# Weighted copies and normalisation products of an attention kernel: from VectorE to GpSimd, with 66 in place of 67 rows and a new order

## The chip, the cores and the metric

The kernel runs on one core of a Trainium2 chip. The metric is the device time of the whole program in microseconds, lower is better; times are medians over several executions. Durations and waits come from one profiled execution. The engines are called as in the profile: PE (TensorE, matrix products; PEld is its loading of weights), ACT (ScalarE), DVE (VectorE), POOL (GpSimd) and SP (SyncE, which here issues DMAs); ACTq and SPq are the engines' sequencers issuing DMAs.

## The reference

A block of multi-head attention: 2048 positions, width 448, 16 heads of 28.

```python
def reference(x, wqkv, wo):
    B, S, D = x.shape
    H = 16
    Dh = D // H
    qkv = (lambda x, *d: x.transpose(*d))((x @ wqkv).reshape(B, S, 3, H, Dh), 2, 0, 3, 1, 4)
    q, k, v = qkv[0], qkv[1], qkv[2]
    scores = jnp.einsum("bhqd,bhkd->bhqk", q, k) * (Dh ** -0.5)
    p = _softmax(scores, axis=-1)
    o = jnp.einsum("bhqk,bhkd->bhqd", p, v)
    return (lambda x, *d: x.transpose(*d))(o, 0, 2, 1, 3).reshape(B, S, D) @ wo
```

All inputs are bfloat16.

## The kernel before, in words

**Tiles, rows, units.** The 16 heads are four groups `g` of four; the 2048 queries are four chunks `c` of 512. A pair (g, c) is a *unit*; there are 16, in the order g then c, so units 12 to 15 are the last group. Within a unit the keys are 16 blocks `kt` of 128. A *tile* is the scores of 128 keys by 512 queries of one head (one PSUM bank); four tiles, one for each head of the group, are a *row*. So there are 256 rows of four tiles, numbered 16 u + kt.

**Two ways to an exponential.** Most tiles go to ACT, which reads two or three banks at once and writes exponentials in bfloat16 to `PT` (line 966). The rows named in `PLAN["rows"]` (line 347) go to DVE in place of that: PE computes each of the four tiles into a bank of its own, DVE turns it into an int16 whose bits, read as a 16-bit float, are a first approximation of the exponential (`DY`, `row_tile`, line 928), and two more instructions over the whole row add a constant phase each (`DS`, line 936). The three are summed with weights 1, 101/128 and 80/128. PE does that sum in the product with V: where a row of ACT needs one pass over V, a row of DVE needs three, the first with `V` and the others with the weighted copies `VW` of it (line 871, function `pv`). The copies are made per group and quarter of the keys, two instructions each (lines 857 to 862): 4 x 4 x 2 = 32 in all. `VW` holds two groups, so a third group's copies wait for the last readers of the first (`vw_used`).

**Banks.** Five of the eight PSUM banks alternate between a three-wide and a two-wide group for ACT, and the tiles for ACT are dealt out 3, 2, 3, 2 and so on (lines 639 to 663). The end of the list is cut so that the last item is one tile wide, in a bank of its own (lines 660 to 663). The other three banks (pool "M", line 508) carry everything else: the sum over V of the current unit, the tiles for DVE, the projections, the output projection.

**End of a unit** (`post_unit`, line 719). DVE copies the sum from PSUM to `OTS` (line 723). The row sums of the softmax are one of its columns; they go by two small DMAs through memory into another layout (L1, L2, lines 729 and 731), DVE takes reciprocals (line 733), and two more DMAs (L3, L4, lines 735 and 737) bring these back, repeated over the partitions, into `RB`. Then `OTS` is multiplied by `RB` into `OTN` (line 739, on the engine `NMENG`, line 372). This holds for units 0 to 13. Unit 14 (`norm_pe`) and unit 15 (`last_unit`) spread the reciprocals with PE and multiply on DVE. When the unit belongs to the last group, four output tiles of its chunk follow: four products with `wop` (line 710), an evacuation (line 696 on ACT, line 698 on DVE) and a store (line 700). Of the last unit's four tiles, 12 to 15, ACT evacuates 12 and 14, DVE 13 and 15; the store of a tile that ACT evacuated is issued by ACT, the others by SP.

**The order.** Every engine executes one list, written out by a planner when the program is built (`_Prog.schedule`, line 125). It takes each operation with its dependencies, a booked duration (`dur`), a priority (`prio`) and, where needed, a bank, and simulates the engines. `CFG` (line 344) holds its settings and `PLAN` the rows and the priorities ("late") of the projections of later groups. Once the lists stand, each engine runs its own strictly in order and waits on semaphores where a producer is on another engine. Where PE has nothing to do the planner puts in products with zeros (line 484).

Beside all this stands a second, general version of the kernel, entered only if a check on the reciprocals fails; it isn't run with these inputs.

Of the kernel before, what the change touches and what calls it, by code (L numbers as in the profile page):

```python
# [63 lines left out]
class _Prog:  # L64
# [276 lines left out]
ZLO = -ZADD  # L341


CFG = {"late": 4.5, "load": 1.5, "load0": 18, "dcost": 2.3, "dlead": 30.385592406, "aslack": 235.147215477, "opp": 0.0, "oload": 2.5, "klead": 0.405674492, "vlag": 0.024622608, "hot1": 45000.0, "hotm": 3600.0, "nslack": 2585.717981114, "dlook": 20.0, "plook": 471.074451806, "rcost": 4.9, "rlead": 1.0, "rend": 4, "rgap": 2, "acost": 0.4455, "dprio": 0.651412491, "nride": 4, "rslack": 300.0, "stail": 24, "jprio": -0.750113813, "sdlap": 4.771128299, "vwlead": 1.249363626, "sdpen": 6.528606395, "rcostx": -0.000676632}

PLAN = {
    "rows": [9, 14, 16, 24, 26, 28, 33, 38, 41, 50, 53, 54, 57, 61, 62, 70, 72, 77, 80, 84, 88, 95, 97, 98, 103, 107, 109, 111, 113, 117, 123, 125, 131, 135, 138, 139, 141, 148, 149, 152, 162, 163, 164, 165, 169, 176, 177, 179, 180, 187, 189, 190, 193, 199, 200, 207, 211, 212, 213, 215, 222, 229, 231, 234, 235, 244, 248],
    "late": [1.281070854, 1.964014751, 1.915657661, 0.76, 2.743900482, 1.159356603, 1.904466413, 1.845975994, 2.106524837, 2.189415295, 2.428349574, 2.873971098, 2.728623137, 3.84085501, 2.733578841, 4.131340808, 3.508351422, 5.446684044, 4.832243098, 4.46548081, 5.163206443, 7.002171665, 6.90767575, 7.804407036, 4.947925744, 6.78739139, 5.302922841, 6.89552453, 9.777227448, 10.389677342, 7.735503962, 7.490566717, 8.23514301, 7.360578973, 7.83742904, 10.319692841, 8.329224918, 8.680463746],
}


def _fast(nc, x, wqkv, wo, out, n_heads=16):
# [9 lines left out]
    NK = NST  # L362
    QCH = 512
    NCH = S // QCH
    NQT = QCH // 128
# [3 lines left out]
    NDR = 3  # L369
    NDS = 3  # L370
    NPH = len(PHASE)
    NMENG = "dve"
    NOB = 4
    scale = float(DH) ** -0.5
    VONE = DH
# [5 lines left out]
    of = out.rearrange("b s d -> (b s) d")  # L381
# [4 lines left out]
    P = _Prog()  # L386
    es = ExitStack()
    with es:
# [66 lines left out]
        def dma_of(t, g):  # L455
# [12 lines left out]
        def zero_pass(acc_open, t):  # L468
# [12 lines left out]
            def emit(e):  # L481
                ins = None
                for h in range(4):
# [13 lines left out]
                       deps=[id_f_op], dur=100, prio=-6, name="sel")  # L497
# [34 lines left out]
        xt_ev = {}  # L532
# [29 lines left out]
        v_ev, vw_ev, vw_used = {}, {}, {}  # L562
# [55 lines left out]
        rows = PLAN["rows"]  # L618
# [73 lines left out]
        def out_tile(n, opm, hold, eng, pr):  # L692
            oi = outs_n[0] % NOB
            outs_n[0] += 1
            if eng == "act":
                fe = (lambda e: e.activation(OUTS[:, oi, :], bank(hold.banks[0])[:, 0:D], AF.Identity))  # L696
            else:
                fe = (lambda e: e.tensor_copy(OUTS[:, oi, :], bank(hold.banks[0])[:, 0:D]))  # L698
            opev = P.add(eng, fe, deps=[opm, outs_last[oi]], dur=550, prio=pr, name=f"OPEV{n}", rel=[(hold, 0)])
            outs_last[oi] = P.add("act" if eng == "act" else "sp", (lambda e: e.dma_start(of[n * 128:(n + 1) * 128, :], OUTS[:, oi, :])),  # L700
                                  deps=[opev], after=[outs_last[oi]], dur=60, prio=pr, name=f"ODMA{n}", dma_group=grp_out[oi],
                                  nbytes=128 * D * 2)

# [15 lines left out]
        def post_unit(u, last_pv):  # L719
# [6 lines left out]
            if u == NU - 2:  # L726
# [10 lines left out]
            l4 = P.add("sp", (lambda e: e.dma_start(RB[:, ub, :], scr_r[u].rearrange("h (o q) -> h o q", o=1).to_broadcast([4, 32, QCH]))),  # L737
                       deps=[l3, ots_last[ub]], dur=400, prio=pr, name=f"L4_{u}", dma_group=grp_l[3 + ub], nbytes=262144, slack=700.0)
            nm = P.add(NMENG, (lambda e: e.tensor_tensor(OTN[:, g, c * QCH:(c + 1) * QCH], RB[:, ub, :], OTS[:, ub, :], ALU.mult)),
                       deps=[l4] + list(xt_ev.values()), dur=1200 if NMENG == "pool" else 610, prio=pr + 0.2, name=f"NM{u}", slack=CFG["nslack"])  # L740
            ots_last[ub] = nm
            finish_unit(g, c, nm, pr)

# [98 lines left out]
        def pv(u, kt):  # L842
# [13 lines left out]

            if r in n_row and (g, kt // 4) not in vw_ev:
                c4 = kt // 4
                vw_ev[(g, c4)] = [P.add("dve", (lambda e, k=k: e.tensor_scalar(VW[:, g % 2, k, 4 * c4:4 * c4 + 4, :], V[:, 4 * c4:4 * c4 + 4, g * 128:(g + 1) * 128],
                                                                              WTERM[k + 1], None, ALU.mult)),  # L860
                                        deps=[v_ev[(g, c4)], vw_used.get((g % 2, c4))], dur=200, prio=u + kt / NK - CFG["vwlead"], name=f"VW{k}_{g}_{c4}")
                                  for k in range(NPH - 1)]

            def weights(k, h):
# [46 lines left out]
        def row_tile(r, h, partner, p_pr):  # L911
# [19 lines left out]
            if len(row_ops[r]) < 4:  # L931
# [2 lines left out]
            rk = n_row[r] % NDS  # L934
            assert n_row[r] < NDS or (n_row[r] - NDS, 1) in row_pv, "DVE rows too close"
            row_ev[r] = [P.add("dve", (lambda e, k=k: e.tensor_scalar(DS[:, k, rk, :], DY[:, ri, :], float(PHASE[k + 1]), None, ALU.add)),  # L936
                               deps=row_ops[r] + [row_pv.get((n_row[r] - NDS, k + 1))], dur=600, prio=pr + 0.001 * k, name=f"DS{k}_{r}") for k in range(NPH - 1)]
            row_at[n_row[r]] = row_ev[r]
            done.update(4 * r + j for j in range(4))

# [811 lines left out]
```

## Time and profile before

| | |
|---|---|
| median of 3 runs | 362.63 us (362.26 to 363.6) |
| the profiled execution | 362.26 us |
| its span, first to last instruction | 360.4 us |
| granted PE clock | 1.00 |
| PE busy | 342.2 us |
| ACT busy | 345.5 us |
| DVE busy | 321.8 us, 574 instructions |
| POOL busy | 3.4 us, 9 instructions |
| exponentials on ACT | 303 (151 three-wide, 151 two-wide, one one-wide) |
| rows on DVE | 67 |

A busy share is an average over the whole span. An instruction's duration runs from its start to its end, and neighbours on ACT and DVE overlap, so durations of a group can add up to more than the engine's busy time. Idle time in a line is that of the engine just before the instruction, with what ended it. The chain of work that ended last is followed back from the last instruction, at each step to what released it.

### The profile page before, as it was taken

Reading aid. Unit: us, or ns where it says so; the run is one execution under the profiler, and the core shown is the slowest. Engines: PE = TensorE matmul, PEld = TensorE weight load, DVE = VectorE, ACT = ScalarE, POOL = GpSimd, SP = SyncE. Lnnn points to the kernel's source line nnn. Section 1 sums busy time; section 2 is a strip of 40 time slices with the busy share of each in tenths; the row PEclk is TensorE's granted clock in tenths of the full one; section 3 lists DMA queues with packets and bytes.
Section 4 is the critical chain, followed back from the end, with each engine's and each line's share of the span. In section 5 each row is a group of like instructions: output and inputs, shape, how many; then the busy total and the mean of one; then the engine's idle time right before and its main releaser. Section 6 shows DMA issues by size and latency. Waiting matters only on the chain.

```text
span 360.4 us, 8848 instructions
## 1 busy us (share of the span) xinstructions
PE 342.2 (95%) x3885; PEld 114.4 (32%) x3885; DVE 321.8 (89%) x574; ACT 345.5 (96%) x307; POOL 3.4 (1%) x9
## 2 busy tenths in 40 slices
PE   8999999999999999999999999999998989999996
PEld 4444322332223243223333323332222222234323
DVE  6579999798999999999999998999999999999504
ACT  2999999999999999999999999999999999999992
POOL 3000000000000000000000000000000000000000
PEclk9999999999999999999999999999999999999999
DMA  8600000100100000000000000000000001010201
GB/s 232 152 2 3 2 32 5 32 2 3 33 0 5 32 18 17 2 32 3 20 15 5 31 2 32 3 14 22 29 4 3 20 15 32 16 44 28 78 29 54
DMA packets 13940, 9.91 MB, mean 27 GB/s; under 512 B 7504, under 2 KB 12048, under 8 KB 13896
## 3 DMA queue, kind: packets, MB, share of 16 engines
q1 hardware_dynamic: 13096, 8.74, 8.4%
q8 instruction: 31, 0.51, 0.6%
q10 hardware_dynamic: 800, 0.56, 0.5%
q14 instruction: 13, 0.11, 0.1%
HBM read 7.23 MB, written 2.06 MB: 26 GB/s over the span
## 4 chain that ended last, share of the span: by engine, by line
ACT 88%; PE 11%; issue 0%; ACTq 0%; DVE 0%
ACT PT L966 87%; PE ps L904 3%; PE ps L871 2%; PE ps L555 2%; PE ps L484 1%; PE ps L789 1%; PE ps L572 0%; PE ps L538 0%; ACT OUTS L696 0%; PE ps L824 0%; PE ps L758 0%; PE ps L809 0%; PE ps L769 0%; PE ps L710 0%; ACT QT L524 0%
## 5 line engine op out<-in xcount | busy, mean ns | idle before, releaser
L966 ACT ACTIVATE PT<-ps 128x1536 bf16<-128x1536 f32 (+1 forms) x303 | 342.5, 1398 | 1.0 <-PE ps L904 0.9
L928 DVE TENSOR_SCALAR DY<-ps 128x512 int16<-128x512 f32 x268 | 175.4, 685 | 9.3 <-PE ps L904 8.1
L904 PE MATMUL ps<-QT,KT 28*128 28x512 bf16 x1024 | 151.6, 384 | 12.9 <-ACT PT L966 8.4
L936 DVE TENSOR_SCALAR DS<-DY 128x2048 int16<-128x2048 int16 x134 | 89.9, 683 | 0.4
L904 PEld LDWEIGHTS ps<-QT,KT 28*128 28x128 bf16 x1024 | 39.7, 91 | 139.0 <-ACT PT L966 101.5
L871 PE MATMUL ps<-PT,V 128*32 128x512 bf16 x756 | 65.8, 385 | 0.7 <-DVE OTS L723 0.4
L871 PE MATMUL ps<-DS,VW 128*32 128x512 f16 x536 | 49.3, 385 | 0.1
L555 PE MATMUL ps<-xT,w_raw 112*32 112x512 bf16 x512 | 35.8, 381 | 0.0
L484 PE MATMUL ps<-ZM,ZW 128*32 128x512 bf16 x324 | 29.5, 410 | 1.2 <-DVE ZM L466 1.2
L871 PE MATMUL ps<-DY,V 128*32 128x512 f16 x268 | 26.5, 385 | 0.1
L871 PEld LDWEIGHTS ps<-PT,V 128*32 128x32 bf16 x756 | 17.1, 94 | 28.4 <-issue 21.9
L871 PEld LDWEIGHTS ps<-DS,VW 128*32 128x32 bf16 x536 | 12.5, 94 | 20.5 <-issue 13.7
L572 PE MATMUL ps<-w_raw,xT 112*128 112x112 bf16 x256 | 17.1, 214 | 0.0
L555 PEld LDWEIGHTS ps<-xT,w_raw 112*32 112x32 bf16 x512 | 12.2, 95 | 13.1 <-issue 3.8
L698 DVE CAST OUTS<-ps 128x448 bf16<-128x448 f32 x14 | 8.6, 622 | 7.6 <-PE ps L710 7.2
L572 PEld LDWEIGHTS ps<-w_raw,xT 112*128 112x128 bf16 x256 | 13.0, 98 | 6.7 <-issue 4.7
L528 DVE CAST KT<-ps 128x512 bf16<-128x512 f32 x16 | 11.0, 689 | 3.5 <-PE ps L555 3.4
L484 PEld LDWEIGHTS ps<-ZM,ZW 128*32 128x32 bf16 x324 | 7.8, 99 | 13.6 <-issue 10.9
L528 DVE CAST V<-ps 128x448 bf16<-128x448 f32 x16 | 9.9, 621 | 2.0 <-PE ps L572 1.9
L526 DVE TENSOR_SCALAR QT<-ps 128x512 bf16<-128x512 f32 x15 | 10.3, 686 | 1.5 <-PE ps L555 1.5
L710 PE MATMUL ps<-wop,XO 128*128 128x448 bf16 x48 | 11.5, 355 | 0.0
L723 DVE COPY OTS<-ps 128x512 f32<-128x512 f32 x15 | 10.3, 687 | 0.5 <-PE ps L871 0.5
(49 smaller groups left out, 79.2 us busy)
## 6 DMA issues: line engine op xcount, KB each, us to landing
RB<-scr_r SPq DMA_DIRECT2D x14, 256.0 KB
out_dram<-OUTS SPq DMA_DIRECT2D x14, 112.0 KB, 1.7
XO<-in_x_dram SPq DMA_DIRECT2D x3, 448.0 KB, 6.3
w_raw<-in_wqkv_dram SPq DMA_DIRECT2D x5, 196.0 KB, 6.3
wop<-in_wo_dram SPq DMA_DIRECT2D x16, 24.5 KB
XO<-in_x_dram SPq DMA_DIRECT2D x1, 224.0 KB, 3.5
XO<-in_x_dram ACTq DMA_DIRECT2D x1, 224.0 KB, 4.0
scr_l<-OTS SPq DMA_DIRECT2D x14, 8.0 KB
```

The costliest lines, as they stand in the source:

```text
L484: ins = e.matmul(ps[32 * h:32 * h + 32, b * 512:(b + 1) * 512], ZW[:, :], ZM[:, :], start=shut, stop=shut, skip_group_check=not shut, tile ...
L526: fe = (lambda e: e.tensor_scalar(evac[0](), evac[1](hold[0].banks[0]), mul, None, ALU.mult))
L528: fe = (lambda e: e.tensor_copy(evac[0](), evac[1](hold[0].banks[0])))
L555: ins = e.matmul(ps[32 * h:32 * h + 32, b * 512:(b + 1) * 512], w_raw[0:IT, it, col:col + 32], xT[0:IT, it, c * 512:(c + 1) * 512], start= ...
L572: ins = e.matmul(ps[:, b * 512 + j * GD:b * 512 + (j + 1) * GD], xT[0:IT, it, n * 128:(n + 1) * 128], w_raw[0:IT, it, 2 * D + g * GD:2 * D ...
L710: return e.matmul(bank(hold[0].banks[0])[:, 0:D], OTN[:, gg, n * 128:(n + 1) * 128], wop[:, gg, :], start=(gg == 0), stop=(gg == G - 1))
L723: accev = P.add("dve", (lambda e: e.tensor_copy(OTS[:, ub, :], bank(pv_open[u].banks[0]))), deps=[last_pv, ots_last[ub]], dur=610, prio=pr ...
L871: ins = e.matmul(ps[32 * h:32 * h + 32, b * 512:(b + 1) * 512], weights(k, h), p_[h], start=(kt == 0 and k == 0), stop=(kt == NK - 1 and k ...
L904: ins = e.matmul(bank(b), KT[32 * h:32 * h + rows, g, kt * 128:(kt + 1) * 128], QT[32 * h:32 * h + rows, g, c * QCH:(c + 1) * QCH], start= ...
L928: o1 = P.add("dve", (lambda e, ri=ri, h=h, s=s: e.tensor_scalar(DY[:, ri, h * 512:(h + 1) * 512], bank(s.banks[0]), ZLO, ZADD, ALU.max, AL ...
L936: row_ev[r] = [P.add("dve", (lambda e, k=k: e.tensor_scalar(DS[:, k, rk, :], DY[:, ri, :], float(PHASE[k + 1]), None, ALU.add)), deps=row_ ...
L966: ex = P.add("act", (lambda e, p0=p0, w=w, bf=bf: e.activation(PT[:, p0 * 512:(p0 + w) * 512], bank(bf(), w), AF.Exp, scale=ESCALE)), deps ...
```

## The change

- The 32 weighted copies `VW` are issued by POOL, and booked by the planner at 790 ns where it booked 200 on DVE. Their priority is another (`vwlead` -0.87 for 1.25).
- `NMENG` is "pool": the 14 products of the normalisation of units 0 to 13 are issued by POOL, booked at 1400 ns (610 on DVE).
- The shifts `DS` are booked at 640 ns, which were booked at 600.
- 66 rows go to DVE, which were 67; most of the row numbers differ, and so do the priorities of the later projections and some settings of the planner. So each engine's list is another.
- Of the stores of tiles that ACT evacuated, ACT issues only those with number 2 modulo 4 (tile 14); the store of tile 12 is issued by SP.

What is computed for each tile is the same; which of the tiles take DVE's approximation differs.

```diff
-CFG = {... "dlead": 30.385592406, "aslack": 235.147215477, ... "klead": 0.405674492, "vlag": 0.024622608, ... "nslack": 2585.717981114, ... "plook": 471.074451806, ... "dprio": 0.651412491, ... "jprio": -0.750113813, "sdlap": 4.771128299, "vwlead": 1.249363626, "sdpen": 6.528606395, ...}
+CFG = {... "dlead": 36.731738807, "aslack": 233.771975282, ... "klead": 0.52957864, "vlag": 0.01121507, ... "nslack": 3486.791836197, ... "plook": 471.336819277, ... "dprio": 0.496462543, ... "jprio": -1.886354641, "sdlap": 4.998836118, "vwlead": -0.865375259, "sdpen": 10.320950691, ...}
...
-    "rows": [9, 14, 16, 24, 26, 28, 33, 38, 41, 50, 53, 54, 57, 61, 62, 70, 72, 77, 80, 84, 88, 95, 97, 98, 103, 107, 109, 111, 113, 117, 123, 125, 131, 135, 138, 139, 141, 148, 149, 152, 162, 163, 164, 165, 169, 176, 177, 179, 180, 187, 189, 190, 193, 199, 200, 207, 211, 212, 213, 215, 222, 229, 231, 234, 235, 244, 248],
+    "rows": [10, 12, 18, 19, 23, 28, 32, 36, 41, 42, 50, 51, 55, 63, 66, 71, 72, 80, 88, 90, 91, 93, 99, 101, 102, 108, 109, 112, 114, 122, 126, 128, 132, 134, 140, 142, 148, 150, 158, 160, 163, 165, 166, 171, 174, 178, 179, 182, 186, 188, 189, 196, 198, 204, 205, 208, 217, 218, 219, 223, 225, 232, 234, 235, 244, 245],
...
-    NMENG = "dve"
+    NMENG = "pool"
...
-            outs_last[oi] = P.add("act" if eng == "act" else "sp", (lambda e: e.dma_start(of[n * 128:(n + 1) * 128, :], OUTS[:, oi, :])),
+            outs_last[oi] = P.add("act" if eng == "act" and n % NQT == 2 else "sp", (lambda e: e.dma_start(of[n * 128:(n + 1) * 128, :], OUTS[:, oi, :])),
...
-                       deps=[l4] + list(xt_ev.values()), dur=1200 if NMENG == "pool" else 610, prio=pr + 0.2, name=f"NM{u}", slack=CFG["nslack"])
+                       deps=[l4] + list(xt_ev.values()), dur=1400 if NMENG == "pool" else 610, prio=pr + 0.2, name=f"NM{u}", slack=CFG["nslack"])
...
-                vw_ev[(g, c4)] = [P.add("dve", (lambda e, k=k: e.tensor_scalar(VW[:, g % 2, k, 4 * c4:4 * c4 + 4, :], V[:, 4 * c4:4 * c4 + 4, g * 128:(g + 1) * 128],
+                vw_ev[(g, c4)] = [P.add("pool", (lambda e, k=k: e.tensor_scalar(VW[:, g % 2, k, 4 * c4:4 * c4 + 4, :], V[:, 4 * c4:4 * c4 + 4, g * 128:(g + 1) * 128],
...
-                                        deps=[v_ev[(g, c4)], vw_used.get((g % 2, c4))], dur=200, prio=u + kt / NK - CFG["vwlead"], name=f"VW{k}_{g}_{c4}")
+                                        deps=[v_ev[(g, c4)], vw_used.get((g % 2, c4))], dur=790, prio=u + kt / NK - CFG["vwlead"], name=f"VW{k}_{g}_{c4}")
...
-                               deps=row_ops[r] + [row_pv.get((n_row[r] - NDS, k + 1))], dur=600, prio=pr + 0.001 * k, name=f"DS{k}_{r}") for k in range(NPH - 1)]
+                               deps=row_ops[r] + [row_pv.get((n_row[r] - NDS, k + 1))], dur=640, prio=pr + 0.001 * k, name=f"DS{k}_{r}") for k in range(NPH - 1)]
```

More of the change, by code (lines that the diff above doesn't have):

```diff
@@ L341 @@
 ZLO = -ZADD
[L344 removed]
+CFG = {"late": 4.5, "load": 1.5, "load0": 18, "dcost": 2.3, "dlead": 36.731738807, "aslack": 233.771975282, "opp": 0.0, "oload": 2.5, "klead": 0.52957864, "vlag": 0.01121507, "hot1": 45000.0, "hotm": 3600.0, "nslack": 3486.791836197, "dlook": 20.0, "plook": 471.336819277, "rcost": 4.9, "rlead": 1.0, "rend": 4, "rgap": 2, "acost": 0.4455, "dprio": 0.496462543, "nride": 4, "rslack": 300.0, "stail": 24, "jprio": -1.886354641, "sdlap": 4.998836118, "vwlead": -0.865375259, "sdpen": 10.320950691, "rcostx": -0.000676632}
@@ new lines @@
+    "late": [1.303310467, 1.41662567, 1.226620141, 1.306204678, 3.072493257, 1.329242951, 1.367188627, 2.038730196, 2.433490174, 2.645350844, 2.255671733, 2.501253065, 2.639666834, 3.573088635, 2.744141229, 4.171940056, 3.434007795, 5.636769061, 5.380683589, 3.297594194, 4.203193172, 6.799614536, 6.596608024, 6.83260115, 5.085198405, 6.271869029, 6.067897092, 5.966707902, 10.321416021, 10.536062226, 7.594374619, 7.031837143, 7.74772636, 7.945146693, 9.152273999, 9.521702491, 9.604656669, 8.019148344],
```

1 line of the change is left out of this document (removed).

## The prediction

> **What bounds the kernel now.** The page's first part gives ScalarE (ACT) 96% of the span. A share is an average, so the next question is what ACT waits for while it runs its exponentials (line 966), and whether the chain of work that ended last passes through them. Behind the page's line, the first fence is the grouping by line with shapes apart, in the stretch from the first exponential to the last but one: count, busy us, mean ns, then idle us in front of the group and its releaser. The second is three pieces of the chain in order of time: start, length, what.
>
> ```profile
> PE 342.2 (95%) x3885; PEld 114.4 (32%) x3885; DVE 321.8 (89%) x574; ACT 345.5 (96%) x307; POOL 3.4 (1%) x9
> ```
>
> ```profile
> L966 ACT ACTIVATE PT<-ps 128x1536 bf16<-128x1536 f32 x151 | 243.2, 1611 | 1.0 <-PE ps L904 0.9
> L966 ACT ACTIVATE PT<-ps 128x1024 bf16<-128x1024 f32 x151 | 179.6, 1189 | 0.0
> ```
>
> ```profile
> 9.42 153.86 ACT PT L966 x136
> ...
> 188.24 43.04 ACT PT L966 x38
> ...
> 235.98 92.83 ACT PT L966 x82
> ```
>
> Exponentials overlap in the engine's pipe, so their mean durations do not add up to time. The pace comes from the chain: 136 exponentials, alternately three and two tiles wide, are 68 pairs of 5 tiles, so 153.86 us over 340 tiles is 452.5 ns per tile; 92.83 us over 205 tiles is 452.8. The pace is the same in both, and in the whole train ACT waits 1.0 us. ACT is the bound from 9.42 us to the last exponential, and nothing done on another engine can take more than that 1.0 us out of the train.
>
> VectorE (DVE) comes second. Next are the busy time by stretch (length, busy us, count), for all its work and then for line 936 alone; its groups by line; and, from the view of line 904 (the score products), what TensorE (PE) sat idle for in front of them and who waited for them.
>
> ```profile
> 14.00:335.00 321.00, 305.25 (x538) 1.00 0.06 17
> ```
>
> ```profile
> 14.00:335.00 321.00, 89.76 (x134) 1.00 0.06 17
> ```
>
> ```profile
> L928 DVE TENSOR_SCALAR DY<-ps 128x512 int16<-128x512 f32 x268 | 175.4, 685 | 9.3 <-PE ps L904 8.1
> L936 DVE TENSOR_SCALAR DS<-DY 128x2048 int16<-128x2048 int16 x134 | 89.9, 683 | 0.4
> L739 DVE TENSOR_TENSOR XO<-RB,OTS 128x512 bf16<-128x512 f32 x14 | 9.6, 684 | 0.0
> L859 DVE TENSOR_SCALAR VW<-V 128x512 bf16<-128x512 bf16 x32 | 8.2, 287 | 0.2
> ```
>
> ```profile
>   DVE DY L928: 15.7, 40
> ...
>   ACT PT L966: 0.9, 2
> ```
>
> Between 14 and 335 us DVE is busy for 95% of the time. It works at nearly the same rate as ACT, but where it is late the cost is small: PE waits 40 times, 15.7 us in all, for DVE to clear a bank, and the exponentials see 1.0 us. Of a wait of PE for DVE, ACT so far feels 1.0/15.7, or 6%.
>
> **The change, part by part.**
>
> *One row fewer on DVE.* A row is four score tiles. The list falls from 67 to 66, so ACT gets 1024 - 264 = 760 tiles where it had 756. 756 tiles are 151 pairs and one single; 760 are 152 pairs, of which lines 660 to 663 split the last two-wide item into two singles. That adds one three-wide and one one-wide instruction: four tiles and two instructions. A tile more costs 1611 - 1189 = 422 ns; a pair takes 5 x 452.6 = 2263 ns, less 5 x 422 = 2110, which leaves 77 ns per instruction. The sum is 4 x 422 + 2 x 77 = 1842 ns, all on the engine that bounds. **+1.84 us**. By the pace alone it would be 4 x 452.6 = 1.81.
>
> *Work taken off DVE.* 14 products of the normalisation (9.6 us), 32 weighted copies (8.2 us), and the row's four conversions and two shifts, 4 x 0.685 + 2 x 0.683 = 4.1 us: 21.9 us of 305. DVE was not the bound, so the gain is only what ACT waits for now: between 0 and 1.0 us. I take nothing here, and keep -1.0 as the low end. PE also loses two passes of four products per row, which ends no wait of ACT.
>
> *Work put on POOL.* No elementwise work of POOL stands in this trace, so I bound it: below by the durations on DVE, 8.2 + 9.6 = 17.8 us; above by POOL's own rows.
>
> ```profile
> L493 POOL MEMSET V<- 128x256 bf16 x1 | 1.2, 1237 | 0.1
> L492 POOL MEMSET V<- 128x1024 bf16 x1 | 1.0, 951 | 0.0
> ```
>
> The dearer of them takes 1237 ns for 256 strided elements: 2.47 us for 512, and twice that, 4.95, where two inputs are read, so 32 x 2.47 + 14 x 4.95 = 148 us. The planner of the change books 790 and 1400 ns, 44.9 us together, which lies between. I take that. Either way it fits into an engine that is busy for 3.4 us. The Trainium skill's GPSIMD Engine Reference, section 3.1, has an addition of two tensors 1.96 times slower than on DVE; that would be an estimated 1.34 us for a product, and the sum below would stay as it is.
>
> What hides it is slack. Here are a V evacuation with its copies on DVE, the first product that uses any copy, and the products with the issue that feeds the last of them.
>
> ```profile
> 27.88 0.62 DVE L528 CAST V<-ps 128x448 bf16<-128x448 f32 x1
> 28.54 0.49 DVE L859 TENSOR_SCALAR VW<-V 128x512 bf16<-128x512 bf16 x2
> ```
>
> ```profile
> L871 PEld LDWEIGHTS ps<-DS,VW x536: 92/93/97, 34.0 to 347.0; 128*32 128x32 bf16 x179
> L871 PE MATMUL ps<-DS,VW x536: 379/389/392, 34.2 to 347.2; 128*32 128x512 f16 x179
> L859 DVE TENSOR_SCALAR VW<-V x32: 281/286/295, 13.8 to 206.9; 128x512 bf16<-128x512 bf16 x32
> ```
>
> ```profile
> 319.92 0.55 SPq L737 DMA_DIRECT2D RB<-scr_r  x1
> ```
>
> ```profile
> 326.77 0.68 DVE L739 TENSOR_TENSOR XO<-RB,OTS 128x512 bf16<-128x512 f32 x1
> ```
>
> The copies of a V that is ready at 28.5 us are first used at 34.0: 5.5 us, against 1.6 for a pair on POOL, or 4.9 at the upper bound. The last copy is made at 206.9, long before its group's first unit (12, at about 9.4 + 12 x 21.4 = 266). A product on POOL waits for its reciprocals (L4, line 737), and copies queued behind it in POOL's order wait too; the first copies come before any product, and later ones are made units ahead. Products of units 0 to 11 are read only by the output projections of the last head group and by the buffer of the unit two later. Those of units 12 and 13 feed projections soon after; 0.7 us later at 326.8, or 4.3 at the bound, is covered by DVE's idle time at the end (6.38 us ahead of line 801, in the next fence). If that cover went, the excess would stand at the end of the span.
>
> *POOL beside DVE.* Line 936 writes 2048 elements in 683 ns, where line 928 writes 512 in 685, so it moves four at a time, and it fills 89.76/321 = 28% of the body. If POOL and such an instruction keep each other out, 46 x 0.28 = 13 of POOL's instructions meet one, and DVE waits on average for half a POOL instruction, 0.49 us: 6.3 us, well below the 21.9 that DVE has been given. At 6% ACT feels 0.40 us. Ends: -1.0 us (DVE never late again) and +4 us (the rival below). **+0.40 us**, by the row of PE's waits, the nearest one.
>
> *The store of tile 12.* It moves from ACT's queue to SP's. The end of the span:
>
> ```profile
> 348.58 3.87 ACT L966 ACTIVATE PT<-ps 128x1024 bf16<-128x1024 f32 x4
> 348.84 0.39 PE L904 MATMUL ps<-QT,KT 28*128 28x512 bf16 x3
> ...
> 352.96 0.76 DVE L801 COPY OTS<-ps 128x256 f32<-128x256 f32 x2 [6.38 <-PE ps L871]
> ...
> 356.42 0.54 ACT L696 ACTIVATE OUTS<-ps 128x448 bf16<-128x448 f32 x1 [3.97 <-PE ps L834]
> ...
> 356.60 0.54 PE L834 MATMUL ps<-wop,XO 128*128 128x448 bf16 x2
> 356.61 1.19 DVE L698 CAST OUTS<-ps 128x448 bf16<-128x448 f32 x2 [0.41 <-PE ps L834]
> 357.00 0.38 ACTq L700 DMA_DIRECT2D out_dram<-OUTS  x1
> ...
> 357.26 0.90 SPq L700 DMA_DIRECT2D out_dram<-OUTS  x2
> 357.47 0.54 ACT L696 ACTIVATE OUTS<-ps 128x448 bf16<-128x448 f32 x1 [0.51 <-PE ps L1007]
> ...
> 358.05 0.35 ACTq L700 DMA_DIRECT2D out_dram<-OUTS  x1
> ```
>
> The named releaser of ACT's second evacuation is not what held it: its product is over by 357.14, while ACT's queue issues the first store until 357.38. Without that issue it starts at 357.0 to 357.14, and its store 0.33 to 0.47 us earlier than 358.05. Then the store of tile 15 is last. DVE clears that tile at 356.61 + 1.19 = 357.80, and SP, with one more store in front, gets to it between 357.80 and 357.90 (three at 0.45 from 357.00 to 358.35). The end moves by 0 to 0.25 us. **-0.25 us**.
>
> *The order anew.* Every engine's order changes with the list of rows, so small stalls fall elsewhere. The fullest unit falls from 7 rows (unit 11) to 6 (units 10 and 11), so I add nothing for it.
>
> **Sum.** The profiled execution took 362.26 us (span 360.4 and 1.9 around it): 362.26 + 1.84 - 0.25 + 0.40 = **364.25 us**. The median before is 362.63, 0.37 above the profiled run; against it this is +0.45%, just inside the half per cent that a measurement of this kernel can tell from no change (360.82 to 364.44).
>
> **Rivals.**
>
> *POOL's holds reach ACT (slower).* PE takes its work in order, so a score product for DVE that waits for a bank holds up the next one for ACT. A two-wide exponential lasts 2 x 422 + 77 = 921 ns; the products for the next need 0.39, so some 0.5 us of PE's lateness is hidden. The rival decides where DVE is held for more than that: about half of the 13 meetings, each passing on some 0.3 us, are 2 us; if POOL's instructions take twice what is booked, 4. With +3: 362.26 + 1.84 - 0.25 + 3 = 366.85. For it speaks that DVE is 95% busy and that POOL's durations are unknown; against it, that DVE gets 21.9 us of room and that 15.7 us of waits cost 1.0. The Trainium skill has a rule for this: SBUF — State Buffer, section "Who interferes with whom", says that a DVE instruction in a two-port mode and a GpSimd one exclude each other, the later one blocking fully for the whole of the other. By that rule the meetings are real. No POOL work stands beside line 936 here, so this trace can't show it.
>
> *ACT's last stalls go (not slower).* With DVE free, the 1.0 us goes: 362.26 + 1.84 - 0.25 - 1.0 = 362.85. The last score products are then never late. Against it: new waits on a new engine.
>
> *A product blocks the copies behind it in POOL's queue.* If L4 lands later than planned, PE waits for copies and ACT stands. One wait of the 6.9 us between issue and product above, less the 5.5 of cover and 0.5 of PE, is about 1; four groups could give 4: 368.
>
> *Faster.* Below 360.8 the time can't come by the train; the 9.42 us in front of it or the 7.9 between its end (348.58 + 3.87) and that of the span would have to shrink by 2. No row shows how.
>
> **Chances.** My forecast 0.54 (its own range 362.8 to 364.9), POOL's holds 0.26, the last stalls gone 0.10, the blocked queue 0.05, faster 0.05. The forecast splits at 364.44 into 0.46 within and 0.08 above. Faster 0.05; within 0.5% 0.46 + 0.10 = 0.56; slower 0.08 + 0.26 + 0.05 = 0.39. For 8 in 10 the range runs from 362.6 to 367.2, which cuts off the upper part of POOL's holds, most of the blocked queue and the faster case.
>
> **What would show it.** 305 exponentials (two one tile wide), and a train about 1.8 us longer at the same 452 ns per tile; DVE busy some 22 us less; ACT's idle time in front of line 966 between 0 and 2 us; the second ACT evacuation at the end starting right behind the first. The forecast is wrong if line 966 waits for several us on PE; if those waits stand beside POOL instructions and longer gaps at line 936, it was POOL's holds; if PE waits for copies, the queue. It is wrong the other way if the pace per tile falls.

## The result, and the profile after

The changed kernel takes 364.52 us (median of 7 runs); the kernel before, timed on the same chips, 362.32 us. The ratio is 1.0052, interval 1.0036 to 1.0069: slower by half a per cent, 2.2 us. One of the seven executions of the changed kernel took 374.94 us at a granted PE clock of 0.96; the ratios, here and below, leave such executions out. The profiled execution took 364.61 us with a span of 362.8, which is 2.4 us above that of before.

First the page's line of busy times, the exponentials by shape, and the view of tile `PT`, whose row gives the shortest, middle and longest duration and then the start of the first and of the last exponential; the last fence is that row for the kernel before.

```profile
PE 343.2 (95%) x3917; PEld 114.6 (32%) x3917; DVE 311.5 (86%) x522; ACT 347.9 (96%) x309; POOL 72.5 (20%) x55
```

```profile
L966 ACT ACTIVATE PT<-ps 128x1536 bf16<-128x1536 f32 x152 | 240.2, 1580 | 1.6 <-PE ps L904 1.2
L966 ACT ACTIVATE PT<-ps 128x1024 bf16<-128x1024 f32 x151 | 175.2, 1160 | 0.0
...
L966 ACT ACTIVATE PT<-ps 128x512 bf16<-128x512 f32 x2 | 1.2, 722 | 0.0
```

```profile
L966 ACT ACTIVATE PT<-ps x305: 716/1337/1767, 9.2 to 354.2; 128x1536 bf16<-128x1536 f32 x152, 128x512 bf16<-128x512 f32 x1
```

```profile
L966 ACT ACTIVATE PT<-ps x303: 728/1338/1768, 9.4 to 351.7; 128x1536 bf16<-128x1536 f32 x151, 128x512 bf16<-128x512 f32 x1
```

That row splits the 2.4 us. The lead in front of the first exponential is 0.2 shorter. The train, from first start to last, is 345.0 us where it was 342.3: +2.7. What follows the last start is 362.8 - 354.2 = 8.6 where it was 360.4 - 351.7 = 8.7. Of the 2.7 us, 1.84 are the additional tiles: one more three-wide exponential and one more single. The other 0.9 is waiting. The starts show it: from a three-wide exponential to the next start it is 1331 ns, from a two-wide one 904 (medians in the traces of both kernels), and what the train holds beyond these is 4.8 us before and 5.7 after. ACT's idle time in front of line 966, 1.0 us before and 1.6 after, shows less of it, because a start can be late while the exponential before it still runs (a three-wide one lasts 1611 ns on average before and 1580 after). The length of the train is the measure of all that follows, since it leaves out the lead, which lay between 9.0 and 9.8 us in the profiled executions without any edit to it. It comes from one execution of each kernel.

Now DVE and POOL: groups by line, the shifts' shortest, middle and longest duration, DVE's busy time between 14 and 335 us, and PE's waits in front of the score products.

```profile
L928 DVE TENSOR_SCALAR DY<-ps 128x512 int16<-128x512 f32 x264 | 172.6, 682 | 16.9 <-PE ps L904 15.6
L936 DVE TENSOR_SCALAR DS<-DY 128x2048 int16<-128x2048 int16 x132 | 94.0, 725 | 0.5
...
L859 POOL TENSOR_SCALAR VW<-V 128x512 bf16<-128x512 bf16 x32 | 49.7, 1554 | 115.6 <-DVE V L528 100.2 <-PE ps L871 14.0
...
L739 POOL TENSOR_TENSOR XO<-RB,OTS 128x512 bf16<-128x512 f32 x14 | 19.5, 1396 | 138.3 <-DMA RB<-scr_r 133.6 <-PE ps L904 4.7
```

```profile
L936 DVE TENSOR_SCALAR DS<-DY x132: 622/683/1665, 25.9 to 336.8; 128x2048 int16<-128x2048 int16 x132
```

```profile
14.00:335.00 321.00, 291.43 (x479) 1.00 0.05 16
```

```profile
  DVE DY L928: 22.0, 58
```

A copy takes 1554 ns on POOL on average where the planner books 790, a product 1396 where it books 1400, and POOL stands idle between them, waiting for V or for `RB`. DVE's body falls by 13.8 us. The typical shift is as fast as before, but the longest takes 1665 ns, where the kernel before has this row:

```profile
L936 DVE TENSOR_SCALAR DS<-DY x134: 628/686/696, 26.1 to 334.4; 128x2048 int16<-128x2048 int16 x134
```

That makes 132 x (725 - 683) ns, 5.5 us, of holds in all. PE waits longer for DVE than before (22.0 us for 15.7) although DVE does less. Most of that comes with the new order and not with the holds: in e2 below, where POOL has none of this work, they are 24.2 us by the same row. One of the held shifts, in the timelines of DVE, POOL and ACT:

```profile
288.25 1.67 DVE L936 TENSOR_SCALAR DS<-DY 128x2048 int16<-128x2048 int16 x1
```

```profile
288.10 1.27 POOL L739 TENSOR_TENSOR XO<-RB,OTS 128x512 bf16<-128x512 f32 x1 [16.67 <-DMA RB<-scr_r]
```

```profile
290.74 5.97 ACT L966 ACTIVATE PT<-ps 128x1536 bf16<-128x1536 f32 x5 [0.49 <-PE ps L904]
```

The product starts at 288.10; the shift that DVE starts 0.15 us later ends 1.0 us late; the next exponentials wait 0.49 us for PE. The end of the span answers to the last step of the prediction:

```profile
358.94 1.11 ACT L696 ACTIVATE OUTS<-ps 128x448 bf16<-128x448 f32 x2 [3.97 <-PE ps L834]
360.08 0.38 ACTq L700 DMA_DIRECT2D out_dram<-OUTS  x1
```

```profile
359.51 1.30 SPq L700 DMA_DIRECT2D out_dram<-OUTS  x3
```

ACT's two evacuations now run one behind the other, and SP issues three stores.

### The profile page after: what moved, and what is told of

Its sections match the earlier page's. It is cut to its first block, busy times and chain, and to the rows that moved or that the text cites. A ratio compares the mean times of both kernels' runs of the same rounds, so it can differ in the third digit from the quotient of the medians.

```text
span 362.8 us, 8936 instructions
## 1 busy us (share of the span) xinstructions
PE 343.2 (95%) x3917; PEld 114.6 (32%) x3917; DVE 311.5 (86%) x522; ACT 347.9 (96%) x309; POOL 72.5 (20%) x55
## 4 chain that ended last, share of the span: by engine, by line
ACT 77%; PE 13%; DVE 6%; DMA 2%; issue 1%; SPq 0%
ACT PT L966 77%; PE ps L904 4%; DVE DY L928 3%; PE ps L871 3%; PE ps L710 3%; DVE DS L936 2%; DMA XO<-in_x_dram 2%; PE ps L789 1%; PE ps L484 1%; DVE OUTS L698 1%; PE ps L758 0%; PE ps L769 0%; PE ps L824 0%; PE ps L809 0%; SPq L444 0%
## 5 line engine op out<-in xcount | busy, mean ns | idle before, releaser
L928 DVE TENSOR_SCALAR DY<-ps 128x512 int16<-128x512 f32 x264 | 172.6, 682 | 16.9 <-PE ps L904 15.6
L936 DVE TENSOR_SCALAR DS<-DY 128x2048 int16<-128x2048 int16 x132 | 94.0, 725 | 0.5
L859 POOL TENSOR_SCALAR VW<-V 128x512 bf16<-128x512 bf16 x32 | 49.7, 1554 | 115.6 <-DVE V L528 100.2
L871 PE MATMUL ps<-PT,V 128*32 128x512 bf16 x760 | 64.8, 385 | 0.9 <-DVE QT L526 0.4
L739 POOL TENSOR_TENSOR XO<-RB,OTS 128x512 bf16<-128x512 f32 x14 | 19.5, 1396 | 138.3 <-DMA RB<-scr_r 133.6
L484 PE MATMUL ps<-ZM,ZW 128*32 128x512 bf16 x364 | 32.9, 404 | 1.2 <-DVE ZM L466 1.2
L555 PEld LDWEIGHTS ps<-xT,w_raw 112*32 112x32 bf16 x512 | 12.5, 95 | 13.8 <-issue 4.1
L484 PEld LDWEIGHTS ps<-ZM,ZW 128*32 128x32 bf16 x364 | 9.1, 98 | 14.5 <-issue 11.7
L526 DVE TENSOR_SCALAR QT<-ps 128x512 bf16<-128x512 f32 x15 | 10.3, 685 | 3.9 <-PE ps L555 3.9
```

The lines of the kernel that those rows point to most:

```text
L484: ins = e.matmul(ps[32 * h:32 * h + 32, b * 512:(b + 1) * 512], ZW[:, :], ZM[:, :], start=shut, stop=shut, skip_group_check=not shut, tile ...
L555: ins = e.matmul(ps[32 * h:32 * h + 32, b * 512:(b + 1) * 512], w_raw[0:IT, it, col:col + 32], xT[0:IT, it, c * 512:(c + 1) * 512], start= ...
L859: vw_ev[(g, c4)] = [P.add("pool", (lambda e, k=k: e.tensor_scalar(VW[:, g % 2, k, 4 * c4:4 * c4 + 4, :], V[:, 4 * c4:4 * c4 + 4, g * 128:( ...
L871: ins = e.matmul(ps[32 * h:32 * h + 32, b * 512:(b + 1) * 512], weights(k, h), p_[h], start=(kt == 0 and k == 0), stop=(kt == NK - 1 and k ...
L928: o1 = P.add("dve", (lambda e, ri=ri, h=h, s=s: e.tensor_scalar(DY[:, ri, h * 512:(h + 1) * 512], bank(s.banks[0]), ZLO, ZADD, ALU.max, AL ...
```

## The experiments

**Theory A:** the number of tiles on ACT sets the time, and POOL's holds of the shifts cost ACT little. **Rival B:** the loss is POOL's doing. To take the parts asunder, the lists must not be planned anew, since another plan has other stalls. So in several kernels the planner runs as it stands, and only then operations are moved between two finished lists, at the start that was planned for them:

```diff
         P.schedule()
+        names = {...}
+        for op in [o for o in P.order["dve"] if o.name in names]:
+            P.order["dve"].remove(op)
+            op.eng = "pool"
+            P.order["pool"].append(op)
+        P.order["pool"].sort(key=lambda o: o.t0)
```

All ratios are to the kernel before on the same chip. "Beyond the count" is the train less 342.3 us and less what the additional or missing tiles make at the prediction's prices (1.84 us for 760 tiles, -1.77 for 752, -3.60 for 748). A star marks a profiled execution with a dip of PE's granted clock, about 1 us longer than its kernel's median; part of the train's excess is that dip.

| kernel | tiles | train, us | beyond the count | median, us | ratio (interval) |
|---|---|---|---|---|---|
| before | 756 | 342.3 | 0 | 362.2 to 362.5 | 1 |
| changed | 760 | 345.0 | +0.9 | 364.52 | 1.0052 (1.0036 to 1.0069) |
| e1 before, copies and products on POOL | 756 | 343.7 | +1.4 | 363.26 | 1.0030 (1.0013 to 1.0047) |
| e2 changed, both back on DVE | 760 | 346.5* | +2.4* | 364.96 | 1.0064 (1.0048 to 1.0081) |
| e3 before, store edit | 756 | 342.3 | 0 | 362.12 | 0.9992 (0.9982 to 1.0001) |
| e4 before, 67 copies more on POOL | 756 | 342.9 | +0.6 | 362.58, one run | |
| e5 before, copies on POOL | 756 | 342.3 | 0 | 362.35 | 1.0005 (0.9993 to 1.0017) |
| e6 before, products on POOL | 756 | 345.0* | +2.7* | 363.79 | 1.0034 (1.0015 to 1.0053) |
| e7 68 rows, both on POOL | 752 | 342.8 | +2.3 | 362.27 | 0.9994 (0.9982 to 1.0006) |
| e8 changed, products back on DVE | 760 | 345.0 | +0.9 | 365.13 | 1.0084 (1.0071 to 1.0097) |
| e9 as e1, products in halves | 756 | 342.8 | +0.5 | 362.81 | 1.0020 (1.0008 to 1.0033) |
| e10 as e7, products in halves | 752 | 341.5 | +1.0 | 361.56 | 0.9978 (0.9968 to 0.9987) |
| e11 69 rows, products in halves | 748 | 339.2 | +0.5 | 360.47 | 0.9938 (0.9918 to 0.9959) |
| e12 changed, products in halves | 760 | 344.4 | +0.3 | 364.29 | 1.0045 (1.0029 to 1.0060) |

**e1: POOL's part alone.** The loop above on the kernel before, with the 32 copies and 14 products in `names`.

> The kernel before with its 67 rows and its planned order; only the 32 weighted copies and the 14 products of units 0 to 13 are taken out of DVE's list and put on POOL's, sorted by the same planned start. Theory A (the time follows the number of tiles on ACT; POOL's holds of the shifts cost ACT a few tenths): 362.3 + 0.4 = 362.7 us, within 362.0 and 363.3, with 303 exponentials and shifts some 40 ns longer on average than 683 ns. Rival B (the 2.2 us of the change are POOL's doing, its holds reach ACT): 364 us or more, with idle time of 3 us or more in front of the exponentials. Rival D (the room given to DVE is worth something by itself): below 362.0.

```profile
L966 ACT ACTIVATE PT<-ps x303: 738/1337/1767, 9.0 to 352.7; 128x1536 bf16<-128x1536 f32 x151, 128x512 bf16<-128x512 f32 x1
```

```profile
L936 DVE TENSOR_SCALAR DS<-DY 128x2048 int16<-128x2048 int16 x134 | 97.2, 737 | 0.4
```

Shifts are 54 ns longer on average, as expected. The cost is 0.3%, more than theory A's 0.4 us (though inside its range, which went to 363.3 us) and less than rival B's 2. By the durations DVE has about 18 us less to do, and the train is longer all the same.

**e2: the plan alone.** The same loop with the two lists exchanged, on the changed kernel.

> The changed kernel with its 66 rows and its planned order; only the copies and the products are put back from POOL's list into DVE's, at their planned start. Theory A: ACT still has 760 tiles, so 364.5 us less the few tenths of POOL's holds, 364.0, and up to 1 us more since DVE has 17.8 us more to do: 363.8 to 365.5. Rival B: with POOL silent the loss goes, 362.3 to 363.0.

```profile
L966 ACT ACTIVATE PT<-ps x305: 725/1338/1767, 9.0 to 355.5; 128x1536 bf16<-128x1536 f32 x152, 128x512 bf16<-128x512 f32 x1
```

Rival B's forecast fails: without any work of POOL the loss is still there (+0.64%). But DVE has more to do here, so e2 doesn't isolate POOL's part. The 2.4 us beyond the count are too much: this execution, at 365.84 us the longest of the six, has a stretch in which PE was granted 0.53 of its clock (the row gives the busy times of PE, PEld, DVE, ACT and POOL and then the clock), and exponentials wait 0.36 and 0.93 us for PE in it.

```profile
79.20:82.80 3.60, 3.60 (x31) 0.75 (x30) 2.75 (x5) 2.32 (x2) 0.00 (x0) 0.53 0.00 0
```

By the medians e2 is 2.5 us slower than the kernel before (364.96 against 362.43 us), so with 1.84 for the tiles, and 0.1 to 0.3 gained by the store, about 0.9 us are stalls, as in the changed kernel.

**e3: the store alone.**

```diff
-            outs_last[oi] = P.add("act" if eng == "act" else "sp", (lambda e: e.dma_start(of[n * 128:(n + 1) * 128, :], OUTS[:, oi, :])),
+            outs_last[oi] = P.add("act" if eng == "act" and n % NQT == 2 else "sp", (lambda e: e.dma_start(of[n * 128:(n + 1) * 128, :], OUTS[:, oi, :])),
```

> The kernel before with one edit: the store of tile 12 is issued by SP and no more by ACT. Theory A: the second evacuation of ACT at the end starts about 0.35 us earlier, the last landing is then that of tile 15, and the time falls by 0.1 to 0.3 us, to 362.1. Rival (the end is set by another store or by the check's flag): no difference, 362.3.

```profile
L966 ACT ACTIVATE PT<-ps x303: 738/1338/1767, 9.2 to 351.5; 128x1536 bf16<-128x1536 f32 x151, 128x512 bf16<-128x512 f32 x1
```

The train is the same, and from the last start to the end of the span (360.0) it is 8.5 us, which was 8.7. The medians differ by 0.31 us, in line with the expected 0.1 to 0.3, but the interval of the ratio just reaches 1.

**e4: POOL beside every shift.** 67 copies that nothing reads, the lists of the other engines unchanged:

```diff
             row_at[n_row[r]] = row_ev[r]
+            P.add("pool", (lambda e: e.tensor_scalar(SCR[:, :], KT[:, 0, 0:416], 0.5, None, ALU.mult)), deps=[row_ops[r][-1], pool_prev[0]], dur=1200, prio=pr, name=f"XP{r}")
+            pool_prev[0] = P.ops[-1]
```

> The kernel before, with the order of PE, ACT, DVE and SP unchanged, and 67 additional copies on POOL (416 elements of KT into a scratch tile that nothing reads), one for each DVE row, started when the row's last conversion is done, so that they run beside the row's shifts. Theory A (a POOL instruction and a shift keep each other out; it was cheap only because DVE had been given room): shifts get several hundred ns longer, some 0.3 to 0.6 us per row pair, 20 to 40 us in all; DVE has only 16 us of idle time between 14 and 335 us, so the time rises by 5 to 25 us. Rival C (no such exclusion; shifts were longer for another reason): shifts stay at 683 ns and the time within 0.5 us of before.

Theory A missed by far. Rival C has the time (362.58 us, one run) but not the shifts, which aren't as before. In this kernel's numbering line 937 is the shift and line 940 the added copy: groups, then the views of the two lines, then three places in the timelines.

```profile
L940 POOL TENSOR_SCALAR SCR<-KT 128x416 bf16<-128x416 bf16 x67 | 105.0, 1567 | 222.9 <-DVE DY L929 222.9
L937 DVE TENSOR_SCALAR DS<-DY 128x2048 int16<-128x2048 int16 x134 | 93.4, 708 | 0.4
```

```profile
L937 DVE TENSOR_SCALAR DS<-DY x134: 621/682/1044, 25.9 to 335.0; 128x2048 int16<-128x2048 int16 x134
```

```profile
L940 POOL TENSOR_SCALAR SCR<-KT x67: 1248/1622/2227, 21.0 to 330.3; 128x416 bf16<-128x416 bf16 x67
```

```profile
105.80 1.50 POOL L940 TENSOR_SCALAR SCR<-KT 128x416 bf16<-128x416 bf16 x1 [1.37 <-DVE DY L929]
...
106.23 0.68 DVE L937 TENSOR_SCALAR DS<-DY 128x2048 int16<-128x2048 int16 x1
```

```profile
57.26 1.25 POOL L940 TENSOR_SCALAR SCR<-KT 128x416 bf16<-128x416 bf16 x1 [1.37 <-DVE DY L929]
```

```profile
121.32 1.61 DVE L937 TENSOR_SCALAR DS<-DY 128x2048 int16<-128x2048 int16 x2
```

```profile
120.68 1.70 POOL L940 TENSOR_SCALAR SCR<-KT 128x416 bf16<-128x416 bf16 x1 [3.69 <-DVE DY L929]
```

The kernel before has a pair of shifts with no POOL instruction near it:

```profile
31.29 1.29 DVE L936 TENSOR_SCALAR DS<-DY 128x2048 int16<-128x2048 int16 x2
```

POOL's instruction spans 1567 ns on average, yet the shifts are only 25 ns longer on average, and none is held for more than 0.36 us. At 106.23 a shift lies wholly inside a copy's span and takes its normal 0.68 us; at 121.32 a pair takes 1.61 us, 0.32 more than the 1.29 of the last row. It is the copies that are longer: the one at 57.26, which meets no shift, takes 1.25 us, the one at 105.80 takes 1.50. Of the 14 copies in this trace whose span no shift overlaps, 11 take 1.25 us; of the 53 others all but one take 1.46 to 2.23. So in these meetings it is mostly POOL that waits, and a copy keeps a shift out for only a part of its span. The step that set the hold at half the span of a POOL instruction had no ground for these copies. For the products it does have one, as the next two experiments show.

**e5 and e6: copies alone, products alone.** From here on theory P says that the length of a single hold decides, so that the products cost and the copies don't; Q says that they don't differ in that. The loop of e1 with only the one kind, then only the other, in `names`.

> The kernel before with its planned order; only the 32 weighted copies are moved to POOL, the 14 products stay on DVE. In the run with both moved, shifts were held up to 1.77 us, and the two stalls of ACT that were new (0.43 and 0.72 us) came some 5 us after holds of 0.9 us at times when a product ran on POOL. Theory P (a product reads two fp32 inputs and holds the shift for about 0.9 us, a copy only 0.4): copies alone cost nothing, 362.3 to 362.7 us, longest shift 1.1 us. Theory Q (the cost comes from copies being late for PE or from the holds of copies): 363 us or more.

> The kernel before with its planned order; only the 14 products of units 0 to 13 are moved to POOL, the copies stay on DVE. Theory P: the products make most of the 0.8 us that both together cost, 362.8 to 363.4 us, longest shift 1.6 us or more, one or two new stalls of ACT of 0.4 to 0.7 us. Theory Q: 362.3 to 362.6.

The train's row and the shifts' row of e5, then of e6:

```profile
L966 ACT ACTIVATE PT<-ps x303: 738/1337/1767, 9.2 to 351.5; 128x1536 bf16<-128x1536 f32 x151, 128x512 bf16<-128x512 f32 x1
```

```profile
L936 DVE TENSOR_SCALAR DS<-DY x134: 625/681/1085, 25.9 to 334.3; 128x2048 int16<-128x2048 int16 x134
```

```profile
L966 ACT ACTIVATE PT<-ps x303: 738/1338/1767, 9.3 to 354.3; 128x1536 bf16<-128x1536 f32 x151, 128x512 bf16<-128x512 f32 x1
```

```profile
L936 DVE TENSOR_SCALAR DS<-DY x134: 624/682/1765, 26.0 to 337.0; 128x2048 int16<-128x2048 int16 x134
```

Theory P fits better, though the intervals of the two ratios just touch. 32 copies on POOL hold a shift for at most 0.40 us and leave the train as it was; 14 products hold one for up to 1.08 us and lengthen it by 2.7 us in the profiled execution (364.81 us, above this kernel's median of 363.79). That is more than theory P had: the ratio puts e6 at 363.4 us, the top of its range, and the median is above it.

How long a product holds a shift can be read from the two starts, here from another place in the changed kernel and from e1:

```profile
304.62 1.27 POOL L739 TENSOR_TENSOR XO<-RB,OTS 128x512 bf16<-128x512 f32 x1 [15.25 <-DMA RB<-scr_r]
```

```profile
304.99 1.45 DVE L936 TENSOR_SCALAR DS<-DY 128x2048 int16<-128x2048 int16 x1
```

```profile
99.41 1.27 POOL L739 TENSOR_TENSOR XO<-RB,OTS 128x512 bf16<-128x512 f32 x1 [17.60 <-PE ps L871]
```

```profile
99.46 1.77 DVE L936 TENSOR_SCALAR DS<-DY 128x2048 int16<-128x2048 int16 x1
```

The shift that starts 0.37 us after its product lasts 0.77 us too long, the one that starts 0.05 after it 1.09, and the one at 288.25 above, 0.15 after it, 0.99. Each time that adds up to about 1.14 us, of the product's 1.27: a shift that meets a product waits for nearly the whole of it.

The worst place of e6, in the timelines of POOL, DVE, PE and ACT and in the busy time of a stretch (PE's granted clock is the 1.00 or 0.57):

```profile
121.72 1.52 POOL L739 TENSOR_TENSOR XO<-RB,OTS 128x512 bf16<-128x512 f32 x1 [21.12 <-DMA RB<-scr_r]
```

```profile
121.42 2.36 DVE L936 TENSOR_SCALAR DS<-DY 128x2048 int16<-128x2048 int16 x2
123.71 0.68 DVE L528 CAST KT<-ps 128x512 bf16<-128x512 f32 x1
```

```profile
124.44 0.54 PE L871 MATMUL ps<-DY,V 128*32 128x512 f16 x4 [1.22 <-DVE KT L528]
```

```profile
125.99 2.54 ACT L966 ACTIVATE PT<-ps 128x1536 bf16<-128x1536 f32 x2 [1.28 <-PE ps L904]
```

```profile
122.00:124.40 2.40, 0.87 (x10) 0.20 (x6) 2.40 (x4) 2.40 (x3) 1.24 (x1) 1.00 0.00 0
124.40:128.40 4.00, 3.96 (x32) 0.78 (x32) 2.59 (x5) 2.65 (x3) 0.00 (x0) 0.57 0.02 3
```

The product falls on the second of a pair of shifts. The evacuation of K behind it is late, PE stands 1.22 us for it, and in the four microseconds after that PE is granted 0.57 of its clock. ACT then waits 1.28 us. How much of that is the hold and how much the clock isn't separated.

**e9 and e12: shorter holds.** Each product is issued as two halves of 256 columns, in e1 and in the changed kernel.

```diff
-            nm = P.add(NMENG, (lambda e: e.tensor_tensor(OTN[:, g, c * QCH:(c + 1) * QCH], RB[:, ub, :], OTS[:, ub, :], ALU.mult)),
+            nm = P.add(NMENG, (lambda e: [e.tensor_tensor(OTN[:, g, c * QCH + o:c * QCH + o + QCH // 2], RB[:, ub, o:o + QCH // 2], OTS[:, ub, o:o + QCH // 2], ALU.mult) for o in (0, QCH // 2)][-1]),
```

> The kernel before with its planned order, copies and products on POOL as in the first experiment (363.26 us), but each product is issued as two halves of 256 columns. Theory P (what reaches ACT is the length of one single hold): no shift is held for more than about 0.6 us, the new stalls go, 362.2 to 362.7 us. Rival (the sum of the holds counts, or a shift waits for both halves): still 363.0 us or more, longest shift 1.6 us or more.

> The changed kernel with its 66 rows and planned order, with each product issued on POOL as two halves of 256 columns and nothing else edited. It takes the long holds away without giving DVE more work, which the run with the products put back on DVE did not. Theory P: the stalls at 292 and 310 us (0.59 and 0.18) go, longest shift 1.25 us or less, 363.6 to 364.1 us against 364.5. Theory Q: 364.3 us or more with stalls of 2 us as before.

```profile
L936 DVE TENSOR_SCALAR DS<-DY x134: 626/683/1237, 26.5 to 335.3; 128x2048 int16<-128x2048 int16 x134
```

```profile
L966 ACT ACTIVATE PT<-ps x305: 725/1337/1767, 9.8 to 354.2; 128x1536 bf16<-128x1536 f32 x152, 128x512 bf16<-128x512 f32 x1
```

The first row is e9's shifts: the longest hold is halved, and of e1's 1.4 us beyond the count 0.5 are left; the median lies 0.45 us below e1's and 0.1 above what theory P had, and the intervals of the two ratios overlap. The second is e12's train, 344.4 us, 0.6 shorter than the changed kernel's, and the last start is at 354.2 in both only because this execution's lead was 0.6 us longer. So, by these two profiles, 0.6 of the 0.9 us in the changed kernel's train are the long holds of products. In the times this shows less clearly: 1.0045 against 1.0052, with intervals that overlap, and 364.29 us misses theory P's 364.1 at most and lies at the 364.3 from which theory Q began. The train is the evidence for theory P here, the median isn't.

**e8: the products back on DVE, in the changed kernel.** The loop of e2 with the 14 products alone.

> The changed kernel with its 66 rows and planned order; only the 14 products are put back into DVE's list, the copies stay on POOL. In the changed kernel the two stalls of ACT at 292.2 us (0.59) and 310.5 us (0.18) came 4 to 5 us after shifts of 1.67 and 1.45 us held by a product. Theory P (only the products' holds reach ACT): these 0.8 us go, so 363.7 us against 364.5, unless the 8.4 us of products on DVE make it late elsewhere, which may take up to 1 us of it back; ACT's train stays 1.8 us longer than before. Theory Q (POOL's holds play no part in the changed kernel): 364.5 us or more.

A miss for theory P; the time is where theory Q had it. The train is 345.0 us as in the changed kernel: the products' holds are gone, but 14 products on DVE at their planned start make as much waiting elsewhere. So e8 can't decide between the two; e12 takes the long holds away without giving DVE anything. The lead was 0.3 us longer in this profile; the rest of the 0.6 us between the medians isn't explained.

**e7, e10 and e11: what the room is good for.** A new order from the same planner, with POOL's work booked as measured (1490 and 1290 ns) and more rows on DVE; e7 has 68 rows, e10 is e7 with halved products, e11 has 69 rows and halves.

> The changed kernel (copies and products on POOL, store of tile 12 by SP) with 68 rows on DVE and a new order from the same planner, which books a copy at 1490 and a product at 1290 ns. ACT has 752 tiles in 302 exponentials. Theory A (tiles on ACT set the time, and POOL's part gives DVE the room for more rows): the train falls by 1.77 us against before and the end by 0.3; with 1 to 2 us of stalls 360.5 to 361.8 us. Rival (DVE or PE can't carry a 68th row, whoever makes the copies): exponentials wait for more than 3 us in all and the time is 363 us or more.

> The kernel with 68 rows and copies and products on POOL (362.27 us), with each product issued as two halves of 256 columns. ACT's train without stalls is 1.77 us shorter than before, and the 68 rows had 3.5 us of stalls where before has 1.2. Theory P: shorter holds take 1 to 2 us of the stalls away, 360.3 to 361.5 us. Rival (the stalls of 68 rows are DVE's or PE's own load): 362.0 us or more.

> Copies and half products on POOL, the store of tile 12 by SP, 69 rows on DVE and a new order from the planner. ACT has 748 tiles; by 2.26 us a pair its train without stalls is 3.6 us shorter than before. Theory A (tiles on ACT set the time, and POOL's work buys rows): with the store's 0.3 us and 1 to 2 us more of stalls than before's 1.2, 359.4 to 360.5 us. Rival (DVE is full at 68 rows): stalls eat the gain, 361.3 us or more.

```profile
L966 ACT ACTIVATE PT<-ps x300: 753/1335/1757, 9.1 to 348.3; 128x1536 bf16<-128x1536 f32 x149, 128x1024 bf16<-128x1024 f32 x1
```

This is e11. e7 missed its expectation by 0.5 us, with 2.3 us of stalls; halves took 1.3 us of those away, and e10, at the edge of its expectation, is faster than before by 0.22%. With 748 tiles e11's train is 3.1 us shorter than that of the kernel before, 3.6 by the count less 0.5 of waiting, and the kernel is faster by 0.62%: 360.47 us against 362.45, the best of all here. It differs from the changed kernel in rows, order and halves. The row count explains its train. But from its last start to the end of the span it has 9.8 us where before had 8.7: behind the last exponential PE has work of its own left, and 1.1 of the 3.1 us come back. Whether another search for an order could do the same with the copies on DVE wasn't tried.

## Why the prediction was right

The median came 0.27 us above the forecast of 364.25, and the likeliest case is the one that came, on the less likely side of its split at 364.44. The closeness is in part luck: the train is 2.7 us longer where the terms make 2.24, and the lead happened to be 0.2 us shorter.

- *One row fewer: right in mechanism and size.* 305 exponentials, two of them one tile wide. In e3, e5, e9, e11 and e12 the train is within 0.5 us of the count, over a range of 12 tiles; in the others it is 0.6 to 2.7 above.
- *DVE's room is worth what ACT waits: taken as nothing, and right in that; the bound was misread.* The low end of -1.0 us took all idle time for waits in the train, and half of that microsecond lay in front of the first exponential, as the timeline of the kernel before has it:

```profile
9.42 5.97 ACT L966 ACTIVATE PT<-ps 128x1536 bf16<-128x1536 f32 x5 [0.49 <-PE ps L904]
```

  On the other hand the starts in the train were 4.8 us late in sum, so idle time was no bound for what could be gained. e5 settles it: with 8.2 us of copies off DVE the train is 342.3 us as before. The sign "DVE busy some 22 us less" didn't come: it is 10.3 less in all and 13.8 in the body, since the holds count as busy and neighbours overlap.
- *POOL's work is covered: right,* though a copy took nearly twice what I took from the diff. PE waits for copies twice in e5, 0.6 us in all, and once in the changed kernel, 0.3; e5's train shows nothing of it.
- *POOL beside DVE: the total held, the way there only in part.* 6.3 us were forecast and 5.5 measured. Half the span is right for the products: the six shifts of the changed kernel that products alone hold lose 0.47 to 0.98 us, on average 0.65 of 1.27. It is too much for the copies (0.4 at most of 1.49), and POOL's work took 69 us where 45 were booked: two errors that cancel, which is luck. The 6% that was to convert it into ACT's time is no constant: with the copies alone it was 0 of 134 x (693 - 683) = 1.3 us (e5's mean is in the row behind this list), with both 1.4 of 134 x (737 - 683) = 7.2 us (e1). What counts, by the trains of e5, e9 and e12, is the length of one hold, which is what the rival had said; its price of 3 us was too high, e12 makes it 0.6. The term was +0.40 and the train's waiting grew by 0.9.
- *The store: right in sign.* -0.25 forecast; from the last start to the end 0.1 less in the changed kernel's profile and 0.2 in e3's, 0.31 between e3's medians, whose interval reaches no change.
- *The order anew: taken as nothing, 0.3 us are left in e12,* where the shorter holds that remain are in it too; they aren't separated. That the order relied on POOL shows in e8.

```profile
L936 DVE TENSOR_SCALAR DS<-DY 128x2048 int16<-128x2048 int16 x134 | 91.3, 693 | 0.4
```

Of the Trainium skill's rule (SBUF — State Buffer, "Who interferes with whom"), the trace agrees that a shift and POOL's instructions can hold each other up: no shift of the kernel before takes more than 696 ns, and in the changed kernel one takes 1665. That the later one waits for the whole of the other is nearly borne out for the products (1.14 of 1.27 us), and isn't for the copies if one takes POOL's reported span for the whole (0.36 us at most in e4, for spans of 1.25 to 2.23). The Trainium skill's Perfetto Trace Analysis, section "GPSIMD Engine Instruction", calls such spans unreliable. e4's copies agree in so far as their span isn't the time for which they keep a shift out.

## What to carry to other kernels

Freeing an engine that the bounding one doesn't wait for gains nothing until the freed time is filled with work taken from the bounding one: the same move to POOL lost 0.5% with 66 rows and, with 69 rows and shorter instructions, won 0.6%. Count first what the change does to the bounding engine's own instructions. Work on an engine that holds up a busy one is, by these trains, best cut into short instructions: fourteen holds of up to a microsecond cost what thirty-two of 0.4 did not.

## What the runs showed of the hardware

- A copy on POOL with one 16-bit input took 1554 ns on average, longer than the product of two fp32 inputs of the same 512 columns (1396), and yet held DVE for less than half as long: 0.40 us at most in e5 against 1.08 in e6.
- A shift that met a product ended about 1.14 us plus its own 0.68 after the product's start, for a product's span of 1.27 (three places above).
- After PE had stood idle for 1.22 us in e6, its granted clock was 0.57 over the next four microseconds. In e2 it was 0.53 over 3.6 us where no wait of PE just before was over 0.45, and in the changed kernel an idle stretch of 0.87 us was followed by a clock of 1.00. So what sets off such a dip isn't shown here.

```profile
289.97 0.40 PE L871 MATMUL ps<-DS,VW 128*32 128x512 f16 x4 [0.87 <-DVE DS L936]
```

- The first exponential started between 9.0 and 9.8 us in executions whose start is the same code (e1 and e9). In the changed kernel's chain of waits that stretch holds a load of x that takes 5.92 us; this spread is in every time here.

```profile
2.23 5.92 DMA XO<-in_x_dram
```
